# Pools begin at multiples of 512 bytes; the odd tile of attention has a place of its own, network items run in halves

## Chip, core and metric

One core of a Trainium2 chip. The metric is the device time of one execution in microseconds, median of three. TensorE (PE) multiplies and transposes, its weight loads (PEld) are recorded by themselves; ScalarE is ACT, VectorE DVE, GpSimd POOL, SyncE SP.

## What is computed

Linear attention without softmax, its result normalised by its root mean square and laid out by token; then two networks behind each other.

```python
kv  = einsum('bhsd,bhse->bhde', k, v)          # 4 x 8 heads, 576 tokens, 64 wide
out = einsum('bhsd,bhde->bhse', q, kv)
x   = out / sqrt(mean(out**2, -1) + 1e-6) * g_norm     # then 2304 tokens x 512
h = x @ w_in                                   # 512 x 2048
x = (h * clip(h + 3, 0, 6) / 6) @ w_out        # 2048 x 512
p = domain_probs / (domain_probs.sum(-1) + 1e-9)
out = sum(p[:, e] * (maximum(x @ w1[e], 0) @ w2[e]) for e in range(4))   # 512 x 1024 x 512
```

## The kernel before

Each matrix product is split: an operand is held as a rounded part and the rest (names with H and L, or index 0 and 1), and three of the four products are summed. Most matmuls have a type of four bytes, F32R; those of the attention are plain F32.

**Attention.** Eight passes `i`, each for half of the heads of one batch. The order of TensorE, ScalarE and VectorE is written out by hand (`manual_schedule`), so each engine runs its instructions in the order of the program text. A pass is:

- `att_out(i)`: products with the transposed q, 32 calls at L241 and 8 at L248, into `pp`, which has three banks of PSUM and one buffer. ScalarE squares them (L253), VectorE sums (L255).
- `att_q(i+1)`: transposes of the next q (L204, L206) into `pq` and `kvp`; ScalarE copies them out (L208, L212).
- `att_rms(i)`: small instructions (L270 to L278), then VectorE scales `pp` into `xt` (L265).
- `att_kv(i+1)`: the next kv, 72 small matmuls (L223); ScalarE copies it four times into `kvd` (L228).
- in passes 3, 5 and 7 a network item: `ff_in`, 12 matmuls of 512 columns into `ph` (L316 to L318), then ScalarE and VectorE by turns (L324, L325, L327, L328). In the other passes there is none.
- `att_x(i-1)`: transposes of the result of the pass before, four tokens' groups at a time into two tiles `px` (L298), and the odd ninth group into `px8` (L301), which is a corner of `pp`. For each of the three ScalarE writes the rounded part `xH` (L290) and VectorE the rest `xL` (L291).
- `conv(SLOTS[i])`: some steps of converting weights of the first network (`convert`, L145 to L166) from raw tiles that SP loads. One half tile is nine steps, ScalarE's or VectorE's.

A last half pass (`i` = 8) has `att_x(7)` alone. `warm(k)` issues matmuls on zeros.

**First network.** `step` issues per item 12 matmuls that stream `xH` or `xL` (L316 to L318) and 12 that stream `gH` or `gL` (L346); 16 features' groups, four blocks of 512 tokens and one of 256. Conversion goes on beside it under a budget.

**Second network.** 48 rounds: `quad` has seven products of six matmuls with 384 columns that stream `xs` (L690), `outs` 36 matmuls with 512 columns that stream `wout` (L657). `sums` is a tile of VectorE's and ScalarE's for them.

PSUM: `psa` has two buffers under one tag for `pq`, `px`, `ph` and zeros; `psx` one for `pq` and `px`; `psk` holds `kvp`.

Places in a partition: pools are laid out from the left and from the right. On the left, behind constants and a pad of `PADL` words, lie `accp` (acc), `gp` (gH, gL), `rp`, `xp` and `xp0` or `xsp` (xH, xL, xs, sums); in the program before they begin 384 bytes past a multiple of 512 (`gp` at 46464, `xsp` at 91520), and all their tiles are multiples of 512 bytes long. On the right lie `wp` (weights, `wout`) and `winp`, which begin at multiples of 512.

Of the kernel before, what the change touches and what calls it, by code (L numbers as in the profile page):

```python
# [17 lines left out]
def kernel(  # L18
# [46 lines left out]
    PADL, PADR = 48, 248  # L65
# [16 lines left out]
    psa = ctx.enter_context(tc.tile_pool(name="psa", bufs=2, space=bass.MemoryType.PSUM))  # L82
# [51 lines left out]
    def convert(n):  # L134
# [4 lines left out]
        for h in range(2):  # L139
# [20 lines left out]
            nc.vector.tensor_tensor(out=r, in0=r, in1=xf, op=ALU.mult)  # L160
            yield 600
            nc.vector.tensor_tensor(out=r, in0=r, in1=a.bitcast(F32), op=ALU.add)
            yield 600
# [27 lines left out]
    px8 = pp[:, NG * D:NG * D + P]  # L191

    def att_q(i):
# [5 lines left out]
        pq = [pool.tile([P, 2, CJ // 2, CP], F32, tag=tag, name="pq") for pool, tag in ((psx, "x"), (psa, "a"))]  # L199
# [15 lines left out]
    def att_kv(i):  # L215
# [4 lines left out]
        for j in range(CJ):  # L220
            for x in range(2):
                for r in range(NP):
                    nc.tensor.matmul(  # L223
                        kvp[half[x ^ r], r, :D], lhsT=t["k"][half[x], r, j, :], rhs=t["v"][half[x], r, j, :],
                        start=(j == 0), stop=(j == CJ - 1))
        for y in range(2):
            for c in range(2):
                nc.scalar.activation(out=kvd[i % 2][half[y], c], in_=kvp[half[c], :, :D], func=AF.Copy)  # L228
# [3 lines left out]
    def att_out(i):  # L232
# [3 lines left out]
        for jj in range(CJ // 4):  # L236
            for r in range(NP):
                for x in range(2):
                    for y in range(2):
# [4 lines left out]
                            rhs=kv[half[y], x ^ r, r], start=True, stop=True)  # L244
# [37 lines left out]
    def att_x(i):  # L282
# [11 lines left out]
        for r, (pool, tag) in enumerate(((psx, "x"), (psa, "a"))):  # L294
            px = pool.tile([P, TB], F32, tag=tag, name="px")
# [15 lines left out]
    def ff_in(u, t, f, later=False):  # L311
        n = BLK[t][1]
        w = W[u, f][:, 0].rearrange("p j (c f) -> p j c f", c=KD)
        ph = psa.tile([P, TB], F32, tag="a", name="ph")[:, :n]
        for c in range(KD):
            nc.tensor.matmul(ph, lhsT=w[:, 0, c, :], rhs=xH[t][:, c, :], start=(c == 0), stop=False)  # L316
            nc.tensor.matmul(ph, lhsT=w[:, 0, c, :], rhs=xL[t][:, c, :], start=False, stop=False)  # L317
            nc.tensor.matmul(ph, lhsT=w[:, 1, c, :], rhs=xH[t][:, c, :], start=False, stop=(c == KD - 1))  # L318
        gH = gp.tile([P, TB], F32R, tag="gH", name="gH")[:, :n]
# [74 lines left out]
    cv = [0, None]  # L394

# [28 lines left out]
    zero = wp.tile([P, DM], mybir.dt.bfloat16, tag=f"w{NW - 1}", name="zero")  # L424
    nc.vector.memset(zero, 0.0)
    zp = psa.tile([P, DM], F32, tag="a", name="zp")

    def warm(k):
        for _ in range(k):
            nc.tensor.matmul(zp, lhsT=zero[:, :P], rhs=zero, start=True, stop=True)  # L430

    warm(8)
# [13 lines left out]
    FILLS = (3, 5, 7)  # L446
    SLOTS = {0: 4, 1: 2, 2: 2, 3: 1, 4: 2, 5: 1, 6: 2, 7: 1, 8: 4}
# [375 lines left out]
```

## Time and profile before

| what | value |
|---|---|
| median of three runs | 1259.22 us (1256.66 to 1260.12) |
| the profiled execution | 1259.21 us |
| its span, first to last instruction | 1257.4 us |
| mean granted clock of TensorE | 0.982 |
| PE, PEld, DVE, ACT, POOL busy | 97%, 85%, 61%, 47%, 0% |

A busy share is the part of the span in which an engine had at least one instruction under way; a granted clock of 1.00 is 2.4 GHz and one of 0.50 is 1.2 GHz. Times are counted from the span's start. The end of a matmul is modelled and overlaps the next one; its pace is read from starts.

### The profile page before, as it was taken

The numbers are of one execution on the slowest core, as the hardware profiler recorded it, in microseconds if no ns is written. First come the engines' busy times: TensorE is split into PE (matmuls) and PEld (weight loads), VectorE is DVE, ScalarE is ACT, GpSimd is POOL, SyncE is SP. The second block draws the span as 40 slices with busy tenths as digits, with TensorE's granted clock in tenths as the row PEclk, the third lists the DMA queues.
The fourth block names the chain that finished last, engine by engine and source line by source line (L and its number), as shares of the span: only waits on it lengthen the run. The fifth ranks groups of instructions, "written<-read, shape, count | busy, mean of one in ns | idle before, by whom it ended". The sixth has DMA issues, their size and how long they took to land.

```text
span 1257.4 us, 16871 instructions
## 1 busy us (share of the span) xinstructions
PE 1225.7 (97%) x6725; PEld 1073.7 (85%) x6725; DVE 773.3 (61%) x1458; ACT 587.0 (47%) x1129; POOL 1.1 (0%) x10
## 2 busy tenths in 40 slices
PE   7879999999999999999999999999999999999997
PEld 5767788888888889999999998999999899999996
DVE  5556999994353375465656576656565856565652
ACT  5546655552232243444444454444444644444441
POOL 0000000000000000000000000000000000000000
PEclk8779999999999999999999999999999999999999
DMA  9421222220010001111212132122222322222202
GB/s 343 142 73 34 84 68 84 84 84 1 1 68 1 1 1 67 35 68 67 68 67 68 68 96 89 68 67 70 71 71 71 91 90 71 72 72 69 72 8 50
DMA packets 59342, 87.13 MB, mean 69 GB/s; under 512 B 3712, under 2 KB 36480, under 8 KB 59264
## 3 DMA queue, kind: packets, MB, share of 16 engines
q1 hardware_dynamic: 59264, 86.07, 20.8%
q8 instruction: 52, 0.85, 0.3%
q14 instruction: 26, 0.21, 0.1%
HBM read 81.34 MB, written 4.72 MB: 68 GB/s over the span
## 4 chain that ended last, share of the span: by engine, by line
PE 94%; DVE 3%; ACT 2%; DMA 0%; issue 0%; SPq 0%; ACTq 0%; DVEq 0%
PE po L657 31%; PE po L346 15%; PE qa L690 14%; PE qb L690 14%; PE ph L316 5%; PE ph L317 5%; PE ph L318 5%; PE pp L241 2%; PE pq L204 1%; DVE xl L291 1%; PE kvp L223 1%; DVE acc L673 1%; ACT kvd L228 0%; ACT acc L360 0%; DMA qin<-in_q_dram 0%; PE pp L248 0%
## 5 line engine op out<-in xcount | busy, mean ns | idle before, releaser
L657 PE MATMUL po<-wout,g 128*128 128x512 f32 x1728 | 400.9, 389 | 0.0
L657 PEld LDWEIGHTS po<-wout,g 128*128 128x128 f32 x1728 | 323.7, 188 | 64.1
L690 PE MATMUL qb<-xs,win 128*128 128x384 f32 x1008 | 204.6, 338 | 1.2 <-ACT us L731 1.2
L690 PE MATMUL qa<-xs,win 128*128 128x384 f32 x1008 | 204.3, 338 | 0.0
L346 PE MATMUL po<-gH,w 128*128 128x512 f32 (+1 forms) x640 | 196.5, 372 | 1.1 <-DVE xl L291 1.1
L690 PEld LDWEIGHTS qb<-xs,win 128*128 128x128 f32 x1008 | 179.2, 188 | 4.0 <-ACT us L731 1.8
L690 PEld LDWEIGHTS qa<-xs,win 128*128 128x128 f32 x1008 | 179.4, 188 | 2.2 <-ACT us L731 0.2
L564 DVE TENSOR_TENSOR wout<-raw,wout 128x512 fp32r<-128x512 f32 x96 | 62.3, 689 | 170.8 <-ACT wout L563 170.8
L563 ACT ACTIVATE wout<-raw 128x512 fp32r<-128x512 f32 x96 | 55.5, 625 | 226.2 <-PE po L657 226.2
L346 PEld LDWEIGHTS po<-gH,w 128*128 128x128 f32 x640 | 116.9, 188 | 24.4 <-DVE xl L291 1.5
L324 ACT ACTIVATE r<-ph,three 128x512 f32<-128x512 f32 (+1 forms) x80 | 51.7, 646 | 153.2 <-PE ph L318 153.2
L316 PE MATMUL ph<-xh,w 128*128 128x512 f32 (+1 forms) x320 | 120.6, 377 | 0.8 <-DVE r L325 0.8
L318 PE MATMUL ph<-xh,w 128*128 128x512 f32 (+1 forms) x320 | 119.9, 375 | 0.0
L317 PE MATMUL ph<-xl,w 128*128 128x512 f32 (+1 forms) x320 | 119.9, 375 | 0.0
L346 PE MATMUL po<-gL,w 128*128 128x512 f32 (+1 forms) x320 | 119.1, 372 | 0.0
L325 DVE SCALAR_TENSOR_TENSOR r<-r,ph 128x512 f32<-128x512 f32 (+1 forms) x80 | 50.6, 632 | 101.1 <-ACT r L324 101.0
L720 DVE SCALAR_TENSOR_TENSOR g<-sums,g 128x384 fp32r<-128x384 f32 x96 | 53.6, 558 | 81.4 <-ACT g L717 81.4
L717 ACT ACTIVATE g<-cs 128x384 fp32r<-128x384 f32 x96 | 50.5, 526 | 64.1 <-DVE cs L733 55.0
L563 ACT ACTIVATE win<-sums 128x512 fp32r<-128x512 f32 x96 | 60.7, 633 | 40.1 <-DVE sums L576 37.7
L316 PEld LDWEIGHTS ph<-xh,w 128*128 128x128 f32 x320 | 60.8, 190 | 13.3 <-DVE r L325 1.2
L318 PEld LDWEIGHTS ph<-xh,w 128*128 128x128 f32 x320 | 60.7, 190 | 12.0 <-DVE w L166 0.4
L317 PEld LDWEIGHTS ph<-xl,w 128*128 128x128 f32 x320 | 60.8, 190 | 11.7
(99 smaller groups left out, 1260.3 us busy)
## 6 DMA issues: line engine op xcount, KB each, us to landing
raw<-in_moe_w_dram SPq DMA_DIRECT2D x96, 512.0 KB, 4.1
raw<-in_moe_w_in_dram SPq DMA_DIRECT2D x16, 512.0 KB, 3.6
raw<-in_moe_w_out_dram SPq DMA_DIRECT2D x16, 512.0 KB, 3.5
qin<-in_q_dram SPq DMA_DIRECT2D x8, 576.0 KB, 4.9
kin<-in_k_dram SPq DMA_DIRECT2D x8, 576.0 KB, 6.1
vin<-in_v_dram SPq DMA_DIRECT2D x8, 576.0 KB, 7.1
out_dram<-acc SPq DMA_DIRECT2D x36, 128.0 KB, 2.3
dp<-in_moe_domain_probs_dram SPq DMA_DIRECT2D x2, 36.0 KB, 5.5
```

The source lines that it names most:

```text
L316: nc.tensor.matmul(ph, lhsT=w[:, 0, c, :], rhs=xH[t][:, c, :], start=(c == 0), stop=False)
L317: nc.tensor.matmul(ph, lhsT=w[:, 0, c, :], rhs=xL[t][:, c, :], start=False, stop=False)
L318: nc.tensor.matmul(ph, lhsT=w[:, 1, c, :], rhs=xH[t][:, c, :], start=False, stop=(c == KD - 1))
L324: lambda: nc.scalar.activation(out=r, in_=ph, func=AF.Relu, bias=three[:, 0:1]),
L325: lambda: nc.vector.scalar_tensor_tensor(out=r, in0=r, scalar=6.0, in1=ph, op0=ALU.min, op1=ALU.mult),
L346: nc.tensor.matmul(po_t[u, t][o], lhsT=lhsT, rhs=rhs, start=(f == 0 and m == 0), stop=(f == UF[u] - 1 and m == 2))
L563: nc.scalar.activation(out=dst[0], in_=src, func=AF.Copy)
L564: nc.vector.tensor_tensor(out=dst[1], in0=src, in1=dst[0].bitcast(F32), op=ALU.subtract)
L657: nc.tensor.matmul(ps[i], lhsT=lhsT, rhs=w[:, f, y], start=(j == 0 and f == 0 and m == 0), stop=(j == FP - 1 and f == 1 and m == 2))
L690: nc.tensor.matmul(bank, lhsT=w[:, wy, AOP[m], c], rhs=xs[m][:, xy, c], start=first and n == 0, stop=n == 5, skip_group_check=True)
L717: nc.scalar.activation(out=g[f][:, 0, t], in_=src, func=func)
L720: nc.vector.scalar_tensor_tensor(out=g[f][:, 1, t], in0=src, scalar=0.0, in1=g[f][:, 0, t].bitcast(F32), op0=ALU.max, op1=ALU.subtract)
```

## The change

`PADL` grows from 48 to 208 words, 640 bytes, so the left pools begin at multiples of 512 bytes; nothing on the right moves. In the attention:

- the odd ninth group is transposed into columns 256 to 383 of the next pass's `kvp`, no longer into `pp` (in the last pass still into `pp`, and the two `px` into `psk`);
- `psa` has two tags: `a1` for `pq` and `px`, `a0` for `ph` and zeros (afterwards `ph` takes both by turns);
- network items for blocks 0 to 2 are issued in halves: six matmuls in an even pass, the other six and the engines' part in the next; passes 0 and 1 have matmuls on zeros there, of the widths in the diff, and zeros are F32R now;
- one copy of the full height and two of half height go to `kvd`, which were four;
- 30 conversion steps in eight passes, which were 19 in nine. In five half tiles the multiply and the add are GpSimd's, in one step;
- the passes are eight; the last `att_x` follows the loop, and the items behind it have another order.

```diff
...
     FMAX = 3.0e38
-    PADL, PADR = 48, 248
+    PADL, PADR = 208, 248
 
...
     rawp = early.enter_context(tc.tile_pool(name="rawp", bufs=3, side="right"))
-    psa = ctx.enter_context(tc.tile_pool(name="psa", bufs=2, space=bass.MemoryType.PSUM))
+    psa = ctx.enter_context(tc.tile_pool(name="psa", bufs=1, space=bass.MemoryType.PSUM))
     attps = ExitStack()
...
             yield 340
-            nc.vector.tensor_tensor(out=r, in0=r, in1=xf, op=ALU.mult)
-            yield 600
-            nc.vector.tensor_tensor(out=r, in0=r, in1=a.bitcast(F32), op=ALU.add)
-            yield 600
+            e = nc.gpsimd if POOLED[0] <= (n, h) < POOLED[1] else nc.vector
+            e.tensor_tensor(out=r, in0=r, in1=xf, op=ALU.mult)
+            if e is nc.vector:
+                yield 600
+            e.tensor_tensor(out=r, in0=r, in1=a.bitcast(F32), op=ALU.add)
+            yield 600 if e is nc.vector else 0
             nc.scalar.activation(out=w[:, h, 0], in_=r, func=AF.Copy)
...
     pp = psp.tile([P, 3 * TB], F32, name="pp")
-    px8 = pp[:, NG * D:NG * D + P]
 
...
         t["q8"] = q8 = qT[:D, 2 * TB:].rearrange("p (r x s) -> p r x s", r=NP, x=2)
-        pq = [pool.tile([P, 2, CJ // 2, CP], F32, tag=tag, name="pq") for pool, tag in ((psx, "x"), (psa, "a"))]
+        pq = [pool.tile([P, 2, CJ // 2, CP], F32, tag=tag, name="pq") for pool, tag in ((psx, "x"), (psa, "a1"))]
         t["kvp"] = kvp = psk.tile([P, NP, TB], F32, tag="k", name="kvp")
...
                         start=(j == 0), stop=(j == CJ - 1))
+        nc.scalar.activation(out=kvd[i % 2][:, 0], in_=kvp[:, :, :D], func=AF.Copy)
         for y in range(2):
-            for c in range(2):
-                nc.scalar.activation(out=kvd[i % 2][half[y], c], in_=kvp[half[c], :, :D], func=AF.Copy)
+            nc.scalar.activation(out=kvd[i % 2][half[y], 1], in_=kvp[half[1 - y], :, :D], func=AF.Copy)
 
...
                             lhsT=t["qm"][half[y], r, x, 2 * jj:2 * jj + 2, :].rearrange("p j s -> p (j s)"),
-                            rhs=kv[half[y], x ^ r, r], start=True, stop=True)
+                            rhs=kv[half[y], x ^ r ^ y, r], start=True, stop=True)
         for x in range(2):
...
 
-    def att_x(i):
+    def att_x(i, pxs, px8):
 
...
 
-        for r, (pool, tag) in enumerate(((psx, "x"), (psa, "a"))):
-            px = pool.tile([P, TB], F32, tag=tag, name="px")
+        for r in range(NP):
+            px = pxs[r]
             for a in range(HH):
...
 
-    def ff_in(u, t, f, later=False):
+    ph_t = {}
+    ph_n = [0]
+
+    def ff_mm(u, t, f, cs):
         n = BLK[t][1]
         w = W[u, f][:, 0].rearrange("p j (c f) -> p j c f", c=KD)
-        ph = psa.tile([P, TB], F32, tag="a", name="ph")[:, :n]
-        for c in range(KD):
+        if cs[0] == 0:
+            ph_t[u, t, f] = psa.tile([P, TB], F32, tag=f"a{ph_n[0] % 2}", name="ph")[:, :n]
+            ph_n[0] += int(done[0])
+        ph = ph_t[u, t, f]
+        for c in cs:
             nc.tensor.matmul(ph, lhsT=w[:, 0, c, :], rhs=xH[t][:, c, :], start=(c == 0), stop=False)
...
             nc.tensor.matmul(ph, lhsT=w[:, 1, c, :], rhs=xH[t][:, c, :], start=False, stop=(c == KD - 1))
+
+    def ff_in(u, t, f, later=False, cs=(0, 1, 2, 3)):
+        n = BLK[t][1]
+        ff_mm(u, t, f, cs)
+        ph = ph_t.pop((u, t, f))
         gH = gp.tile([P, TB], F32R, tag="gH", name="gH")[:, :n]
...
     cv = [0, None]
+    done = [False]
+    POOLED = ((0, 1), (3, 0))
 
...
 
-    zero = wp.tile([P, DM], mybir.dt.bfloat16, tag=f"w{NW - 1}", name="zero")
-    nc.vector.memset(zero, 0.0)
-    zp = psa.tile([P, DM], F32, tag="a", name="zp")
-
-    def warm(k):
-        for _ in range(k):
-            nc.tensor.matmul(zp, lhsT=zero[:, :P], rhs=zero, start=True, stop=True)
-
-    warm(8)
+    zero = wp.tile([P, DM], F32R, tag=f"w{NW - 1}", name="zero")
+    nc.vector.memset(zero.bitcast(F32), 0.0)
+    def warm(sizes):
+        zp = psa.tile([P, DM], F32, tag="a0", name="zp")
+        for n in sizes:
+            nc.tensor.matmul(zp[:, :n], lhsT=zero[:, :P], rhs=zero[:, :n], start=True, stop=True)
+
+    warm([DM] * 8)
 
...
     nc.sync.dma_start(out=gcol[D:2 * D, :], in_=g_norm.rearrange("(p o) -> p o", o=1))
-    FILLS = (3, 5, 7)
-    SLOTS = {0: 4, 1: 2, 2: 2, 3: 1, 4: 2, 5: 1, 6: 2, 7: 1, 8: 4}
+    SLOTS = {0: 3, 1: 3, 2: 4, 3: 4, 4: 4, 5: 4, 6: 4, 7: 4}
     nop = lambda: None
...
         qc = att_q(0)
-        warm(4)
         for x in qc[:2]:
             x()
+        warm([DM] * 6)
         att_kv(0)
         qc[2]()
+        warm([DM] * 2)
         conv(3)
-        for i in range(NHB + 1):
+        for i in range(NHB):
             if i + 2 < NHB:
...
             nxt = i + 1 < NHB
-            if i < NHB:
-                att_out(i)
-                qc = att_q(i + 1) if nxt else [nop] * 3
-                rms = att_rms(i)
-                qc[0]()
-                rms[0]()
-                qc[1]()
-                for x in rms[1:]:
-                    x()
+            att_out(i)
+            qc = att_q(i + 1) if nxt else [nop] * 3
+            rms = att_rms(i)
+            qc[0]()
+            rms[0]()
+            qc[1]()
+            for x in rms[1:]:
+                x()
             if nxt:
...
                 qc[2]()
-            later = fill(True) if i in FILLS else [nop] * 4
-            later[0]()
-            later[1]()
-            em = att_x(i - 1) if i else []
+            fin = [nop] * 4
+            if i < 2:
+                warm(((480,) * 3 + (504,) * 3 + (506,) * 2, (248,) * 3 + (250,) * 3 + (288,) * 3 + (368,) * 3)[i])
+            elif i % 2 == 0:
+                ff_mm(0, i // 2 - 1, 0, (0, 1))
+            else:
+                fin = ff_in(0, i // 2 - 1, 0, later=True, cs=(2, 3))
+            fin[0]()
+            fin[1]()
+            em = []
+            if i:
+                pxs = [pool.tile([P, TB], F32, tag=tag, name="px") for pool, tag in ((psx, "x"), (psa, "a1"))]
+                em = att_x(i - 1, pxs, st[min(i + 1, NHB - 1)]["kvp"][:, 0, 2 * P:3 * P])
             for m, (x, y) in enumerate(em):
...
                 if m == 1:
-                    later[2]()
+                    fin[2]()
                 y()
-            later[3]()
-            if i < NHB:
-                conv(SLOTS[i])
+            fin[3]()
+            conv(SLOTS[i])
+        pxs = psk.tile([P, NP, TB], F32, tag="k", name="px")
+        for x, y in att_x(NHB - 1, [pxs[:, r] for r in range(NP)], pp[:, NG * D:NG * D + P]):
+            x()
+            y()
+        done[0] = True
         attps.close()
         psb = ctx.enter_context(tc.tile_pool(name="psb", bufs=1, space=bass.MemoryType.PSUM, reuse_waits="tile"))
-        for kind, t in (("o", 0), ("o", 1), ("i", 3), ("i", 4), ("o", 2), ("o", 3), ("o", 4)):
+        for kind, t in (("o", 0), ("i", 3), ("o", 1), ("i", 4), ("o", 2), ("o", 3), ("o", 4)):
             if kind == "i":
...
 
-    qa = psa.tile([P, TB], F32, tag="a", name="qa")[:, :TH]
-    qb = psa.tile([P, TB], F32, tag="a", name="qb")[:, :TH]
+    qa = psa.tile([P, TB], F32, tag="a0", name="qa")[:, :TH]
+    qb = psa.tile([P, TB], F32, tag="a1", name="qb")[:, :TH]
     nc.tensor.matmul(qb, lhsT=win[0][:, 0, 0, 0], rhs=xs[1][:, 0, 0], start=True, stop=True)
...
```

## Rows read from the trace of the kernel before

**Rows 1.** The page: granted clock in 40 slices of the span

```profile
PEclk8779999999999999999999999999999999999999
```

**Rows 2.** Stretches: length, busy (count) of PE, PEld, DVE, ACT, POOL; clock, DMA

```profile
20.50:27.30 6.80, 6.80 (x90) 6.14 (x91) 4.24 (x10) 2.48 (x5) 0.00 (x0) 0.50 1.05 395
...
92.20:99.00 6.80, 6.80 (x46) 5.89 (x44) 2.38 (x8) 2.13 (x4) 0.00 (x0) 0.50 0.00 0
...
110.00:300.00 190.00, 189.25 (x881) 154.94 (x880) 167.84 (x317) 99.46 (x169) 0.00 (x0) 1.00 0.24 73
...
300.00:480.00 180.00, 180.00 (x829) 148.08 (x828) 83.72 (x137) 57.19 (x92) 0.00 (x0) 1.00 0.04 12
```

**Rows 3.** Waits between 11.8 and 106 us: total, times, longest

```profile
PE pp L241 <- DVE xl L291: 14.0, 6, 2.6
```

**Rows 4.** One pass in order of time (start, length)

```profile
31.87 2.00 PE L241 MATMUL pp<-kvd,qT 64*128 64x64 f32 x32 [2.63 <-DVE xl L291]
...
34.93 1.41 DVE L255 TENSOR_REDUCE ssq<-xt 128x8 f32<-128x512 f32 x2 [2.51 <-ACT xt L253]
...
37.82 1.42 DVE L265 TENSOR_TENSOR xt<-pp,ri 128x512 f32<-128x512 f32 x2
...
40.47 1.41 DVE L291 SCALAR_TENSOR_TENSOR xl<-px,gcol,xh 128x512 fp32r<-128x512 f32 x2 [1.23 <-ACT xh L290]
...
41.80 0.34 DVE L291 SCALAR_TENSOR_TENSOR xl<-pp,gcol,xh 128x128 fp32r<-128x128 f32 x1
...
42.19 1.00 PE L241 MATMUL pp<-kvd,qT 64*128 64x64 f32 x14 [2.57 <-DVE xl L291]
```

**Rows 5.** TensorE in order of time: first and eighth pass, output products

```profile
11.77 2.65 PE L241 MATMUL pp<-kvd,qT 64*128 64x64 f32 x32 [0.40 <-ACT kvd L228]
...
91.80 3.36 PE L241 MATMUL pp<-kvd,qT 64*128 64x64 f32 x32 [2.35 <-DVE xl L291]
...
106.15 0.50 PE L346 MATMUL po<-gH,w 128*128 128x512 f32 x1 [1.06 <-DVE xl L291]
```

**Rows 6.** TensorE in order of time, second network

```profile
596.79 1.22 PE L690 MATMUL qa<-xs,win 128*128 128x384 f32 x6
...
603.11 8.34 PE L657 MATMUL po<-wout,g 128*128 128x512 f32 x36
...
611.28 1.21 PE L690 MATMUL qa<-xs,win 128*128 128x384 f32 x6
```

**Rows 7.** TensorE in order of time, first network, 512 columns

```profile
380.90 0.39 PE L316 MATMUL ph<-xh,w 128*128 128x512 f32 x1
...
386.48 0.40 PE L316 MATMUL ph<-xh,w 128*128 128x512 f32 x1
```

**Rows 8.** TensorE in order of time, first network, 256 columns

```profile
334.67 0.28 PE L316 MATMUL ph<-xh,w 128*128 128x256 f32 x1
...
336.09 0.39 PE L346 MATMUL po<-gH,w 128*128 128x512 f32 x1
```

**Rows 9.** TensorE's groups by line and shape, the whole span

```profile
L690 PE MATMUL qb<-xs,win 128*128 128x384 f32 x1008 | 204.6, 338 | 1.2 <-ACT us L731 1.2
...
L346 PE MATMUL po<-gH,w 128*128 128x512 f32 x512 | 171.6, 395 | 1.1 <-DVE xl L291 1.1
```

**Rows 10.** VectorE's conversion by line, 11.8 to 106 us: count, busy, mean ns

```profile
L160 DVE TENSOR_TENSOR r<-r,x 128x512 f32<-128x512 f32 x2 | 1.4, 688 | 0.0
...
L158 DVE TENSOR_SCALAR x<-a 128x512 uint32<-128x512 uint32 x2 | 0.9, 428 | 0.1
```

**Rows 11.** TensorE in order of time: instructions at full clock

```profile
14.73 0.66 PE L204 MATMUL pq<-ident,qin 128*128 128x128 f32 x4
...
15.97 1.28 PE L223 MATMUL kvp<-vin,kin 64*64 64x64 f32 x72
...
100.11 1.03 PE L298 MATMUL px<-ident,xt 128*128 128x128 f32 x8
```

**Rows 12.** GpSimd's groups by line, the whole span

```profile
masks.py:199 POOL TENSOR_SCALAR_AFFINE_SELECT ident<-ident 128x128 f32<-128x128 f32 x1 | 0.3, 295 | 0.0
```

## The prediction

> **What bounds the kernel now.** I read the page first [rows 1]: TensorE's granted clock is whole everywhere except in the first three of the 40 slices (31.4 us each; some 100 us in all), the attention. So there are two questions: where the attention loses time, and at what pace TensorE runs behind it, where it never stops. The busy time of each engine by stretches says the same more sharply [rows 2]: behind 110 us TensorE is busy for 189 of 190 us at clock 1.00, although VectorE has 168 of them full too; inside the attention there are seven stretches at clock 0.50, of which the first and the last are shown, together some 41 of the 89 us between 10.3 and 99.0.
>
> The waits of the attention [rows 3] name the cause: TensorE stands for 14.0 us, six times, before L241 (the products of attention, into `pp`) until VectorE's L291 ends. One pass of the loop in order of time shows which L291 [rows 4]. L241 starts at 31.87, VectorE reduces from 34.93 and has scaled the result at 37.82 + 1.42 = 39.24. Then `pp` could be written again, but the odd tile of the pass before is transposed into a corner of `pp`, and its last reader ends at 41.80 + 0.34 = 42.14. L241 starts at 42.19. A pass is 10.32 us long, of which 2.95 are this detour. In the passes with a network item or a cold clock it is longer: between the first and the eighth L241 (11.77 to 91.80 us) lie 80.0 us, 11.4 a pass [rows 5].
>
> Behind the attention I read TensorE's start times. The second network's second product streams 512 columns from `wout`: 36 of them take 611.28 - 603.11 = 8.17 us, 226.9 ns each; its first one streams 384 columns from `xs`: 36 in 603.11 - 596.79 = 6.32 us, 175.6 ns each [rows 6]. The first network, also 512 columns, streams from `xH`, `xL`, `gH` and `gL`: 24 in 386.48 - 380.90 = 5.58 us, 232.5 ns each [rows 7]. Its short block (256 columns) needs 1.42 us for 12, 118.3 ns each [rows 8]. Between 300 and 480 us VectorE is mostly idle, so the 5.6 ns between the two kinds of 512 columns is no matter of VectorE's load. What differs is the moving operand's place: `wout` begins at a multiple of 512 bytes, and the other four 384 bytes past one. Weights begin at multiples in all of them.
>
> **Part 1, the pads.** 640 more bytes put `x`, `g`, `xs` and `sums` on multiples of 512. The trace has no matmul of 384 or 256 columns that streams from such a place, so both are bounded.
> - 512 columns: 1,500 behind the attention (768 of L346 [rows 9], 768 of L316 to L318, less 36), at 5.6 ns: 8.4 us.
> - 384 columns: 2,016 [rows 9]. If time is in proportion to columns, the aligned one takes 226.9 x 384/512 = 170.2, gain 5.4 ns, 10.9 us. If instead the 128 columns fewer save only their 53.3 ns at 2.4 GHz, it takes 173.6, gain 2.0 ns, 4.0 us. I take 7: the 256-column row is below what a fixed cost on top of 2.4 GHz would give (226.9 - 106.7 = 120.2), so proportion is nearer.
> - 256 columns: 384, between 0 and 118.3 - 113.5 = 4.8 ns: 0 to 1.8 us, I take 1.
>
> The sum is 16.4 us, between 12.4 and 21.1. TensorE is the bound there, so all of it counts; VectorE's 168 of 190 us leave room for steps 2.4% shorter.
>
> One rule of the Trainium skill speaks against this part: "TensorE: Matmul & The Clock Gate", section "Back-to-back issue gap", gives the gap as columns over 2.4 GHz plus 2.5 ns, from the columns alone (215.8 ns for 512), so by it the shift would bring 0 us. The trace does not agree: 226.9 and 232.5 ns for equal columns.
>
> **Part 2, the odd tile.** It goes into the spare columns of `kvp`, so L241 waits for the scaling alone: a pass can't be shorter than 39.24 - 31.87 = 7.37 us. Late next are two queues.
> - VectorE, in order: reduce to scale 4.31 us and the three L291 1.75 [rows 4]; half of a network item's two instructions (L325, L328) every pass, 0.69, as VectorE's instructions with two tiles of 128x512 take 0.69 [rows 10]; conversion. The slots now give the passes from the third on, by turns, L148, L151, L155 and L158 (three at 0.43 and one at 0.69 [rows 10]) and L166 (0.69), 1.3 on the mean. Sum 8.1; with the gaps between instructions and the waits for ScalarE I take 8.5.
> - TensorE at full clock: L241 2.00 [rows 4] and L248 (eight calls more) some 0.4, transposes and L223 15.97 + 1.28 - 14.73 = 2.52 [rows 11], half a network item 6 x 0.2325 = 1.40, and nine transposes of results some 1.1 (eight take 1.03) [rows 11], 7.4 together. At half clock L241 takes 3.36 [rows 5], with L248 some 4.0, the rest at most twice as long, 14.1 together.
>
> So at full clock VectorE sets the pass at 8.5; TensorE's idle time falls from some 3 us a pass to 1, and the clock, which now falls after each such stop, should hold more often. I put a fifth to a quarter of TensorE's time at half clock, which it partly takes out of its 1 us of slack, and take 9.0 (8.3 to 9.9).
>
> **Part 3, small moves.** Two more warming matmuls come ahead of the first L223 (512 columns at 1.2 GHz: 0.43 us each), two more behind it, where TensorE would wait, and one of four copies to `kvd` falls away: the first L241 moves from 11.77 to some 12.4. The warming matmuls of passes 0 and 1 stand where TensorE would wait. Network items in halves are the same 12 matmuls; as `ph` has a bank of its own during attention, transposes no longer wait for its readers. The 11 more conversion steps are VectorE's, counted above; SP's loads behind them wait for instructions that VectorE has executed a pass earlier.
>
> Five half tiles give their multiply and add to GpSimd. No row shows such an operation there. The nearest is a 128x128 select at 0.30 us [rows 12]: four times that, 1.2 us, for 512 columns; ten of them are 12 us. They take 10 x 0.69 = 6.9 us off VectorE [rows 10], which my 8.1 already leaves out. ScalarE's L164 behind them comes a whole pass later, so 2.4 us are covered. If they hold VectorE up for their whole length, the head is 12 us longer; if never, 0. I take 1, since only the tiny instructions between reduce and scale fall in their time.
>
> The Trainium skill ("SBUF — State Buffer", section "Who interferes with whom") says that a VectorE instruction with two SBUF inputs and a GpSimd one that reads SBUF exclude each other for a whole instruction. No row shows it, as GpSimd does nothing here after 2 us; by it the cost is within those bounds.
>
> **Sum for the attention.** First L241 at 12.4; the first pass 7.7 (no L291 yet), six at 9.0: the eighth at 74.1 instead of 91.80. Behind it, before: 106.15 - 91.80 = 14.35, of which 1.4 already went into six output products, so 12.95. After: scaled at 7.37, L325 0.69, the seventh result's L291 1.75, then the last result (transposes 0.45, ScalarE 0.67, L291 1.75): 12.7. Gain 17.9; less 1 for GpSimd, and 1 that I keep back for a first pass at half clock: 16. Bounds: 9.9 us a pass 12, less a part of GpSimd's: 7; 8.3 a pass: 22.
>
> The profiled execution took 1259.21 us (span 1257.4 and 1.8 around it), the median 1259.22. So 1259.2 - 16.4 - 16 = 1226.8, rounded to 1227; with both bounds 1216 to 1240.
>
> **Rivals.**
> 1. The place of the moving operand is not the cause of the 5.6 ns (`wout` also lies at the other end of a partition, beside its weights). For it: no row of the same tile at two places. Against it: `xH` to `gL` lie far apart and all show some 232 ns. Then the attention alone: 1237 to 1252, about 1243.
> 2. The attention gains little, as the clock stays as it was, VectorE's queue is fuller than I count, or GpSimd holds it up: a pass of 11 us. For it: 41 us at 0.50 now. Then 1259.2 - 16.4 and a few us: 1238 to 1247.
> 3. Neither counts: 1256 to 1262.
> 4. Slower. The clock falls in the attention and does not rise again, since half items and products of 64 columns follow each other without long work. Place: L241 of each pass. Price: 14.1 us a pass instead of 11.4, 7 passes, 19 us: 1278 without a gain behind it, 1262 with it. It decides from 11.4 us a pass on without the pads' gain, and from about 13.7 with it. Against it: in every cold stretch of now the clock rose while TensorE was busy throughout [rows 2].
>
> **Chances.** Both parts as said 0.63, the attention alone 0.17, the pads alone 0.10, neither 0.04, slower 0.06. The likeliest gives 1227. From 1215 to 1248 leaves out rivals 3 and 4, and some of 1: less than 2 in 10. Within 0.3% (3.8 us, about what a measurement here can tell from no change) lies rival 3 and a little of rivals 1 and 4: same 0.06; faster 0.89; slower 0.05.
>
> **What would show it.** Start times of L346 at 227 ns each, of L690 at 170 to 174; L241 starting right behind L265 with `pp` no longer waiting for L291; eight passes of 8.3 to 9.9 us; the first output product between 80 and 92 us; at most two or three cold stretches. Wrong would be: 232 ns unchanged, passes of over 10 us, or ScalarE's L164 waiting for GpSimd.

## The result and the profile after

The changed kernel takes 1239.08 us (median of four runs, 1238.81 to 1240.38), the kernel before 1258.11 (four runs, 1256.66 to 1260.12). The ratio is 0.985, with a 95% interval of 0.9832 to 0.9867: faster by 17 to 21 us. The prediction said 1227 with a range of 1215 to 1248. So the sign and the range held: 19 of the 32 us forecast came, and the time is 12 us above the forecast.

The profiled execution took 1240.38 us (span 1238.6). In it TensorE's clock outside the cold stretches is recorded as 0.95, not 1.00; its matmuls keep the same pace as in executions recorded at 1.00, so 0.95 is read here as the upper level. Granted clock in 40 slices, as [rows 1]:

```profile
PEclk9868999999999999999999999999999999999998
```

The waits between 11.8 and 106 us (engine, line and tile; what it waited for; total, times, longest), as [rows 3]:

```profile
POOL r L161 <- DVE x L158: 87.1, 5, 21.0
...
PE px L299 <- DVE xl L292: 6.0, 1, 6.0
...
ACT w L166 <- POOL r L164: 3.9, 1, 3.9
...
PE po L358 <- DVE xl L292: 3.0, 1, 3.0
...
PE pp L242 <- DVE xt L266: 2.4, 2, 1.3
```

The 14.0 us before the products into `pp` are gone: they wait for the scaling (L266) alone, 2.4 us in all. New are three long single stops: 6.0 us before the last transposes, 3.0 before the first output products, and 3.9 of ScalarE waiting for GpSimd. One pass in order of time, as [rows 4] (L266 scales, L292 writes `xl`):

```profile
27.49 2.01 PE L242 MATMUL pp<-kvd,qT 64*128 64x64 f32 x32
...
33.61 1.42 DVE L266 TENSOR_TENSOR xt<-pp,ri 128x512 f32<-128x512 f32 x2
...
35.08 1.11 PE L242 MATMUL pp<-kvd,qT 64*128 64x64 f32 x16
...
35.15 1.41 DVE L292 SCALAR_TENSOR_TENSOR xl<-px,gcol,xh 128x512 fp32r<-128x512 f32 x2
```

The next L242 starts at 35.08, with the end of the scaling, and L292 comes after it. This pass is 7.59 us long; all seven between the first L242 (11.09) and the eighth (71.71) take 8.66 on the mean, against 11.4 before [rows 5]. The eighth starts 20.1 us earlier than before. TensorE from there on:

```profile
75.53 1.06 PE L299 MATMUL px<-ident,xt 128*128 128x128 f32 x8
76.42 0.28 PE L302 MATMUL kvp<-ident,xt 128*128 128x128 f32 x1
82.69 1.97 PE L299 MATMUL px<-ident,xt 128*128 128x128 f32 x8 [5.99 <-DVE xl L292]
84.45 0.42 PE L302 MATMUL pp<-ident,xt 128*128 128x128 f32 x1
87.83 0.76 PE L358 MATMUL po<-gH,w 128*128 128x512 f32 x1 [2.95 <-DVE xl L292]
```

And two of the four cold stretches between 45 and 121 us (length, busy time and count of PE, PEld, DVE, ACT, POOL; clock; DMA), as [rows 2]:

```profile
62.50:69.40 6.90, 6.90 (x107) 6.13 (x106) 5.94 (x14) 4.77 (x12) 0.00 (x0) 0.50 0.01 2
79.60:93.25 13.65, 7.61 (x22) 6.07 (x23) 7.45 (x14) 5.97 (x11) 0.00 (x0) 0.50 0.13 38
```

The second is the longest of the kernel. TensorE had stood since 76.70, 2.9 us, when at 79.6 the granted clock went to its lower level, 1.2 GHz; the eight transposes then take 1.97 us instead of 1.06 (75.53), and twelve output products 93.08 - 87.83 = 5.25 instead of 12 x 0.2267 = 2.72. Equal matmuls further on show how much was lost: near 124 us the changed kernel is some 10 us ahead, no longer 20. It gets 8 of these back in the first network, and is 17.8 ahead at the second network's first output (a group of three L690 at 508.78 against L715 at 491.00) and 18.9 at the end (1249.09 against 1230.22). So the second network, the longest part, brings 1.1.

Behind the attention, the second network (36 products of 512 columns, and 384-column ones ahead of them), as [rows 6]:

```profile
582.04 1.20 PE L715 MATMUL qb<-xs,win 128*128 128x384 f32 x6
583.08 1.21 PE L715 MATMUL qa<-xs,win 128*128 128x384 f32 x6
...
585.16 8.36 PE L682 MATMUL po<-wout,g 128*128 128x512 f32 x36
593.36 1.23 PE L715 MATMUL qa<-xs,win 128*128 128x384 f32 x6
```

The first network, 24 matmuls of 512 columns from one row to the other, as [rows 7]:

```profile
354.66 0.39 PE L323 MATMUL ph<-xh,w 128*128 128x512 f32 x1
...
360.10 0.39 PE L323 MATMUL ph<-xh,w 128*128 128x512 f32 x1
```

and twelve of 256 columns, as [rows 8]:

```profile
329.78 0.28 PE L358 MATMUL po<-gH,w 128*128 128x256 f32 x1
...
331.22 0.40 PE L323 MATMUL ph<-xh,w 128*128 128x512 f32 x1
```

So 5.44 / 24 = 226.7 ns for 512 columns (232.5 before), 1.04 / 6 = 173.3 for 384 and 1.44 / 12 = 120.0 for 256 (118.3 before). Each 128 columns are 53.3 ns, which is 2.4 GHz, and 13.4 ns lie on top whatever the length. Over all starts the mean of the 384-column matmuls went from 176.6 to 175.4 only, as one in sixteen takes 182 or more, and that of the 512-column ones of `wout` rose from 227.1 to 227.8.

The Trainium skill, "TensorE: Matmul & The Clock Gate", section "Back-to-back issue gap", has 2.5 ns on top of the columns for a single matmul at 2.4 GHz. The trace does not agree: these FP32R streams show 13.4 ns, and the place counts, too.

### The profile page after: what moved, and what is told of

Same layout as the page of the kernel before. It is cut to its first block, busy times and chain, and to the rows that moved or that the text cites. A ratio compares the mean times of both kernels' runs of the same rounds, so it can differ in the third digit from the quotient of the medians.

```text
span 1238.6 us, 16911 instructions
## 1 busy us (share of the span) xinstructions
PE 1209.9 (98%) x6749; PEld 1067.7 (86%) x6749; DVE 769.6 (62%) x1448; ACT 583.4 (47%) x1121; POOL 14.0 (1%) x20
## 4 chain that ended last, share of the span: by engine, by line
PE 93%; DVE 3%; DMA 2%; ACT 1%; issue 0%; SPq 0%; POOLq 0%; POOL 0%; ACTq 0%; DVEq 0%
PE po L682 31%; PE po L358 15%; PE qa L715 14%; PE qb L715 14%; PE ph L323 5%; PE ph L324 5%; PE ph L325 5%; DMA vin<-in_v_dram 1%; DMA kin<-in_k_dram 1%; PE pp L242 1%; DVE acc L698 1%; PE kvp L224 1%; DVE xl L292 1%; PE pq L205 0%; PE px L299 0%; ACT acc L372 0%
## 5 line engine op out<-in xcount | busy, mean ns | idle before, releaser
L715 PE MATMUL qb<-xs,win 128*128 128x384 f32 x1008 | 203.3, 336 | 1.2 <-ACT us L756 1.2
L715 PE MATMUL qa<-xs,win 128*128 128x384 f32 x1008 | 203.0, 335 | 0.0
L715 PEld LDWEIGHTS qb<-xs,win 128*128 128x128 f32 x1008 | 177.9, 188 | 3.8 <-ACT us L756 1.8
L715 PEld LDWEIGHTS qa<-xs,win 128*128 128x128 f32 x1008 | 178.2, 188 | 2.2 <-ACT us L756 0.2
L358 PEld LDWEIGHTS po<-gH,w 128*128 128x128 f32 x640 | 118.3, 190 | 26.3 <-issue 3.3
L323 PE MATMUL ph<-xh,w 128*128 128x512 f32 (+1 forms) x320 | 119.6, 374 | 2.4 <-DVE r L337 2.4
L325 PE MATMUL ph<-xh,w 128*128 128x512 f32 (+1 forms) x320 | 118.3, 370 | 0.0
L337 DVE SCALAR_TENSOR_TENSOR r<-r,ph 128x512 f32<-128x512 f32 (+1 forms) x80 | 50.5, 632 | 101.5 <-ACT r L336 101.2
L323 PEld LDWEIGHTS ph<-xh,w 128*128 128x128 f32 x320 | 61.0, 190 | 13.6 <-DVE r L337 2.9
L745 DVE SCALAR_TENSOR_TENSOR g<-cs,g 128x384 fp32r<-128x384 f32 x96 | 53.3, 555 | 27.2 <-ACT g L742 27.2
```

The lines of the kernel that those rows point to most:

```text
L337: lambda: nc.vector.scalar_tensor_tensor(out=r, in0=r, scalar=6.0, in1=ph, op0=ALU.min, op1=ALU.mult),
L358: nc.tensor.matmul(po_t[u, t][o], lhsT=lhsT, rhs=rhs, start=(f == 0 and m == 0), stop=(f == UF[u] - 1 and m == 2))
L715: nc.tensor.matmul(bank, lhsT=w[:, wy, AOP[m], c], rhs=xs[m][:, xy, c], start=first and n == 0, stop=n == 5, skip_group_check=True)
L745: nc.vector.scalar_tensor_tensor(out=g[f][:, 1, t], in0=src, scalar=0.0, in1=g[f][:, 0, t].bitcast(F32), op0=ALU.max, op1=ALU.subtract)
```

## Experiments

My theory: the operand's place gives some 9 us; the odd tile out of `pp` shortens the passes; and about 10 us are given back at the handover by the stop ahead of the last transposes, by the cold clock that it leaves, and by GpSimd's last half tile. Rivals: it isn't the place but the attention's new order that speeds the stream; the halves and the conversion shorten the passes, not the odd tile; ScalarE and VectorE set the handover, not TensorE's clock. All ratios below are to the kernel before, with 95% intervals.

| run | median us | ratio |
|---|---|---|
| the changed kernel | 1239.1 | 0.985 (0.9832 to 0.9867) |
| e1_before_pad832 | 1250.5 | 0.9949 (0.9929 to 0.9969) |
| e2_before_pad704 | 1255.4 | 0.9995 (0.9973 to 1.0017) |
| e3_before_pad64 | 1250.9 | 0.994 (0.9917 to 0.9962) |
| e8_before_pad128 | 1250.3 | one run |
| e4_after_pad192 | 1246.9 | 0.9921 (0.9896 to 0.9946) |
| e12_before_px8_alone | 1241.2 | 0.9843 (0.9807 to 0.9879) |
| e5_after_px8_back | 1254.1 | 0.9968 (0.9954 to 0.9982) |
| e10_after_whole_items | 1246.3 | 0.9898 (0.9881 to 0.9915) |
| e6_after_gpsimd_to_2_0 | 1233.5 | 0.9806 (0.9784 to 0.9827) |
| e11_gpsimd_none | 1240.1 | 0.9855 (0.9838 to 0.9872) |
| e7_after_filled_wait | 1238.6 | 0.985 (0.9833 to 0.9868) |
| e9_gpsimd_filled_own_tiles | 1230.2 | 0.9776 (0.9758 to 0.9793) |

### The pads

```diff
-    PADL, PADR = 48, 248
+    PADL, PADR = 208, 248     # e1 (e2: 176, e3: 16, e8: 32)
```

> The kernel before with one number changed: the left pad has 208 elements instead of 48, so x, g and sums begin at multiples of 512 bytes; attention stays as it was. My theory (a matmul whose moving operand begins off the multiple costs about 6 ns more at 512 columns, 1 to 2 ns more at 384, nothing at 256): 512-column cadence 233 to 227 ns, 384-column 176.5 to 173.5, 256-column unchanged or 1 ns longer, and the time about 1249 us (9 less). Rival, the place is not the cause of the faster cadence (it comes with the attention's new order): about 1258 us.

> The kernel before with a left pad of 176 elements instead of 48: all tiles behind it move by exactly 512 bytes, so that each keeps its remainder to 512. My theory (the remainder counts): no change, 1258 us, 512-column cadence 233 ns. Rival (the amount of the move or the neighbourhood counts, not the remainder): the cadence and the time of the run with 208 elements, about 1249 us.

> The kernel before with a left pad of 16 elements instead of 48: all tiles behind it move down by 128 bytes, to a remainder of 256 to 512. If only the multiple of 512 is free: 1258 us, 512-column cadence 233 ns. If a multiple of 256 is free too: about 1249 us and 227 ns. If the cost grows with what hangs over: between them.

> The kernel before with a left pad of 32 elements: x, g and sums begin 64 bytes beyond a multiple of 256 (before: 128 beyond; the run with 16 elements: on it, at 256 beyond a multiple of 512, and as fast as on the multiple of 512). If only the multiple of 256 is free: a 512-column cadence of 231 to 235 ns. If the remainder's size counts: clearly different from before's 233, in either direction; if 64 is free: 227.

The same 24 matmuls of the first network, in e3:

```profile
382.86 0.39 PE L316 MATMUL ph<-xh,w 128*128 128x512 f32 x1
...
388.30 0.39 PE L316 MATMUL ph<-xh,w 128*128 128x512 f32 x1
```

and in e8:

```profile
383.03 0.39 PE L316 MATMUL ph<-xh,w 128*128 128x512 f32 x1
...
388.52 0.39 PE L316 MATMUL ph<-xh,w 128*128 128x512 f32 x1
```

That is 226.7 and 228.8 ns each on the mean of the 24; e1 has 226.7 (381.19 to 386.63) and e2 232.5 (382.57 to 388.15). So the place is the cause, with the attention untouched, and the amount of the shift isn't: e2 moves everything by 512 bytes and changes nothing. But the multiple is 256, not 512, as e3 shows: 256 bytes past a multiple of 512 is as good. The cost isn't one of on or off either: 128 bytes past a multiple of 256 costs 5.8 ns, 64 bytes past costs 2.1. In e8 the second network even gains more than in the changed kernel (384 columns 174.7 on the mean, `wout`'s 512 columns 227.0, as against 175.4 and 227.8), so that the one run of e8 is as fast as e1 and e3. Why, stays open.

### The attention without the pads

```diff
-    PADL, PADR = 208, 248
+    PADL, PADR = 48, 248
```

> The changed kernel with the left pad of before (48 elements): the attention's part of the change by itself. My theory: 1248 us, that is 10 below the kernel before and 9 above the changed kernel, with the passes of attention as short as in the changed kernel (8.7 us) and the 512-column cadence back at 233 ns. Rival, the place is not the cause: 1239 us.

1246.9 us, 7.8 above the changed kernel, with the pace of before (232.1 to 233.3 ns) and passes of 8.29 us on the mean. The two parts, 6.4 (e1) and 9.9 us (e4, both from the ratios), are 16.3 together, beside 18.9 for the whole; their own intervals, 2.5 and 3.1 us either way, cover the difference.

### The odd tile, alone and put back

On the kernel before (e12) and on the changed one (e5):

```diff
 e12
-    px8 = pp[:, NG * D:NG * D + P]
...
-    def att_x(i):
+    def att_x(i, px8):
...
-            em = att_x(i - 1) if i else []
+            em = att_x(i - 1, st[min(i + 1, NHB - 1)]["kvp"][:, 0, 2 * P:3 * P]) if i else []
 e5
-                em = att_x(i - 1, pxs, st[min(i + 1, NHB - 1)]["kvp"][:, 0, 2 * P:3 * P])
+                em = att_x(i - 1, pxs, pp[:, NG * D:NG * D + P])
```

> The changed kernel with the odd tile's transposes back in the results' tile pp in every pass; the pads and the network items in halves stay. My theory (the move out of pp is what shortens the passes): the wait of L242 for the last xl write returns at 1 to 2 us a pass, a pass takes 10 us or more instead of 8.7, the eighth L242 starts near 81 us instead of 71.7, and the time is about 1248 us. Rival (the halves, and the conversions' place, shorten the passes): passes stay under 9 us and the time under 1242 us.

> The kernel before with one edit: the odd tile's transposes go to the next pass's kvp tile instead of the results' tile pp; pads, network items, conversion's places and engines stay as before. If the move out of pp is by itself what shortens the passes: L241's wait of 14.0 us for the xl writes goes, passes of 11.4 us on average become 9 to 9.5, time about 1244 us (14 less, which is what putting the tile back cost the changed kernel). Rival (the move pays only together with the halves and GpSimd's share, because TensorE then waits without work and falls to half clock, and VectorE's queue is longer): passes of 10 us or more, 1250 us or more.

In e5 the wait is back (the view of waits):

```profile
PE pp L242 <- DVE xl L292: 11.6, 6, 2.1
```

Its eighth L242 starts at 89.09 and its time is 15 us longer than the changed kernel's, more than I had expected. e12 goes further: one edit, with old pads, old items and no GpSimd, gives as much as the whole change as far as the intervals tell (15 to 24 us, the whole change 17 to 21). No L240 (L241 before) waits for an `xl` write any more. TensorE in three of its passes:

```profile
50.09 2.00 PE L240 MATMUL pp<-kvd,qT 64*128 64x64 f32 x32
...
57.52 2.00 PE L240 MATMUL pp<-kvd,qT 64*128 64x64 f32 x32 [0.35 <-DVE xt L264]
...
67.82 2.00 PE L240 MATMUL pp<-kvd,qT 64*128 64x64 f32 x32
...
75.42 2.36 PE L240 MATMUL pp<-kvd,qT 64*128 64x64 f32 x32 [0.35 <-DVE xt L264]
```

7.4 and 7.6 us where the pass has no network item, 10.3 where it has one; the pass with an item ahead of these took 11.77, and all seven take 9.16 on the mean, within the 9 to 9.5 expected. The eighth starts at 75.42 and the first output product at 89.70, later than in the changed kernel (71.71 and 87.83); yet the profiled execution, at 1246.13 us the slowest of its four, has gained 13.5 us by 120 us, against 10. And e12 (1241.2) lies below e4 (1246.9), which has the same pads and everything else of the change besides; their intervals don't meet. So by the medians the rest of the attention's part, taken together, costs time; the two profiled executions don't show it, as e4's has gained 14.2 us by 120 us. The next runs take the rest apart.

### The halves of the network items

```diff
             elif i % 2 == 0:
-                ff_mm(0, i // 2 - 1, 0, (0, 1))
+                pass
             else:
-                fin = ff_in(0, i // 2 - 1, 0, later=True, cs=(2, 3))
+                fin = ff_in(0, i // 2 - 1, 0, later=True)
```

> The changed kernel with the network items whole in passes 3, 5 and 7, as in the kernel before, and none in passes 2, 4 and 6. My theory (VectorE's queue sets the pass, TensorE has some 1 us to spare, so that whole items lengthen an odd pass by less than they shorten an even one): the passes stay at 8.6 to 9 us and the time within 2 us of the changed kernel's 1239. Rival (the halves carry the clock and the passes): TensorE cold in the passes without an item, passes of 9.5 us or more, time 1243 us or more.

The rival won: 1246.3 us. Stretches from one L242 to the next, a pass with a whole item and one without:

```profile
37.40:49.20 11.80, 11.80 (x145) 10.36 (x145) 7.51 (x17) 4.97 (x13) 2.54 (x2) 0.71 0.62 216
49.20:57.50 8.30, 6.46 (x133) 5.33 (x132) 7.28 (x16) 7.87 (x18) 0.00 (x0) 1.00 0.64 223
```

In the second TensorE is busy for 6.46 of 8.30 us, at 1.00; the pass behind such a one begins at half clock (mean 0.71) and takes 11.8 us, TensorE busy throughout. Both kinds together are 10.05 a pass; with the halves the same four passes take 9.16 (35.08 to 71.71). It is the clock: VectorE is busy for only 7.51 of the 11.80. Not all of the 7.2 us between the medians need be the halves: in this profiled execution the first L242 already starts 1.8 us later (12.89 against 11.09), ahead of every pass that the edit touches, and near 130 us it is 6.1 us behind the changed kernel in all.

### GpSimd's half tiles

```diff
 e6
-    POOLED = ((0, 1), (3, 0))
+    POOLED = ((0, 1), (2, 1))
 e11: the same, and
-            e = nc.gpsimd if POOLED[0] <= (n, h) < POOLED[1] else nc.vector
+            e = nc.vector
+            pooled = POOLED[0] <= (n, h) < POOLED[1]
...
-            if e is nc.vector:
+            if not pooled:
                 yield 600
...
-            yield 600 if e is nc.vector else 0
+            yield 0 if pooled else 600
```

> The changed kernel with GpSimd's share ending one half tile earlier, so that the half tile behind the loop over passes, (2, 1), goes back to VectorE. My theory (GpSimd's 2.7 us there delay ScalarE's L166, the copies of the sums behind it, and TensorE): L166's wait of 3.9 us shrinks by about 1.5 us, TensorE's waits near 103 and 117 us (1.6 and 2.5 us) shrink by as much together or more, time about 1236 us (2 to 4 less than the changed kernel). Rival (VectorE loses 1.3 us by it and gives nothing back): 1239 us or more.

> The changed kernel with GpSimd's share ended before (2, 1) and its four other half tiles put on VectorE in the same steps, so GpSimd computes nothing there. Against the run with the share cut alone (1233.5 us): each half tile puts 1.4 us back on VectorE, which my theory has as what sets the pass, so the four passes lengthen by up to 1.4 us each and the time goes to 1235 to 1239 us. Rival (VectorE's small operations are slowed by GpSimd at the same port as much as its work shrinks, or the pass is set elsewhere): 1233 us or less.

GpSimd takes 1.28 us an operation (its groups by line, changed kernel), as estimated:

```profile
L164 POOL TENSOR_TENSOR r<-r,a 128x512 f32<-128x512 f32 x5 | 6.4, 1280 | 0.4
L161 POOL TENSOR_TENSOR r<-r,x 128x512 f32<-128x512 f32 x5 | 6.4, 1278 | 87.1 <-DVE x L158 87.1
```

The last half tile in order of time, changed kernel:

```profile
98.83 0.42 DVE L158 TENSOR_SCALAR x<-a 128x512 uint32<-128x512 uint32 x1
...
99.39 1.29 POOL L161 TENSOR_TENSOR r<-r,x 128x512 f32<-128x512 f32 x1 [21.01 <-DVE x L158]
...
100.77 1.28 POOL L164 TENSOR_TENSOR r<-r,a 128x512 f32<-128x512 f32 x1
...
102.08 0.63 ACT L166 ACTIVATE w<-r 128x512 fp32r<-128x512 f32 x1 [3.89 <-POOL r L164]
```

ScalarE comes to L166 at 98.19 and stands until 102.08; behind it wait the copies of the sums (L372), for these TensorE (1.6 us near 103), and later TensorE again for VectorE's L337 (2.5 us at 117.3), after which its clock is low until 120.6. In e6 VectorE has L164 done at 98.50 + 0.69, ScalarE's L166 follows at 99.22 after a wait of 0.60, and both of TensorE's waits are gone:

```profile
99.22 0.63 ACT L166 ACTIVATE w<-r 128x512 fp32r<-128x512 f32 x1 [0.60 <-DVE r L164]
```

Taking one half tile of five off GpSimd was worth 5.5 us, more than I expected. The other four are better there: e11 is 6.6 us slower than e6. VectorE's queue isn't the only reason: it is longer by 1.4 us in those passes, but three passes take 10.7 to 11.4 us, where e6's take 8.9 (L243, which is L242 here, from 45.26 to 55.97, 67.38 and 78.10). The first and the third of them run at full clock nearly throughout (means 0.95 and 1.00). In them ScalarE stands 2.58 and 2.34 us for VectorE's half tile (L167, which is L166 here; all its waits up to 122 us below), and TensorE behind it 2 us for ScalarE's copies. Only in the one between is the clock low: it fell at 54.8 us, within the first one's stops, and rose at 65.0.

```profile
ACT w L167 <- DVE r L165: 8.9, 5, 2.6
```

### The wait filled, and tiles of their own

```diff
 e7, in the last pass, behind att_x(i - 1) (e9: 18 products)
+            if not nxt:
+                for _ in range(24):
+                    nc.tensor.matmul(st[i]["kvp"][:, 1, :], lhsT=W[0, 0][:, 0, 0, :P],
+                                     rhs=xH[0][:, 0, :], start=True, stop=True)
 e9, behind the loop, with e6's POOLED
-        pxs = psk.tile([P, NP, TB], F32, tag="k", name="px")
-        for x, y in att_x(NHB - 1, [pxs[:, r] for r in range(NP)], pp[:, NG * D:NG * D + P]):
+        pxs = [pool.tile([P, TB], F32, tag=tag, name="px") for pool, tag in ((psx, "x"), (psa, "a1"))]
+        em = att_x(NHB - 1, pxs, pp[:, NG * D:NG * D + P])
+        for _ in range(11):
+            nc.tensor.matmul(pp[:, :TB], lhsT=W[0, 0][:, 0, 0, :P], rhs=xH[0][:, 0, :],
+                             start=True, stop=True)
+        for x, y in em:
```

> The changed kernel with 24 products of 512 columns of real data in TensorE's 6 us of waiting in the last pass, behind the transposes of the result before; they go to the free half of that pass's kvp tile and nobody reads them. My theory (the half clock from 79.6 to 93.3 us comes from that wait and costs the last transposes about 1 us and the first twelve second products 2.3 us): the clock stays up there, L299's eight take 1.1 us instead of 2.0, the twelve products 2.8 instead of 5.1, time about 1236 us (3 less). Rival (what TensorE gains, ScalarE's queue takes back at the copies of the sums): 1239 us.

> The changed kernel with GpSimd's share ending before (2, 1), the last pass's wait filled with 18 products of 512 columns, the gap behind the last transposes filled with 11 more (both into sums that nobody reads), and the last pair of transposed tiles in the two tiles that the other passes use, in place of one shared tile. My theory (the half clock through the handover and the shared tile's waits of 0.8 to 1 us are worth it): against the run with GpSimd's share alone cut (1233.5 us) about 1 us from the last transposes, 2.3 from the first twelve second products and 1 to 1.5 from the tiles, so 1229 us. Rival (ScalarE and VectorE set the handover, TensorE's clock doesn't): 1233 us.

e7 came out at the rival's number. TensorE in order of time:

```profile
77.37 5.72 PE L507 MATMUL kvp<-xh,w 128*128 128x512 f32 x24
83.93 1.09 PE L299 MATMUL px<-ident,xt 128*128 128x128 f32 x8 [0.84 <-DVE xl L292]
84.86 0.27 PE L302 MATMUL pp<-ident,xt 128*128 128x128 f32 x1
88.18 0.77 PE L358 MATMUL po<-gH,w 128*128 128x512 f32 x1 [3.05 <-DVE xl L292]
```

The transposes run at full clock (1.09 us), as I said. But behind the next stop, 3.05 us, the output products start at half clock again. And the fill isn't free: ScalarE's read of the odd tile in `kvp` waits 0.82 us for these products, which go to the same tile. From the eighth L242 (72.67) to the first output product it is 15.5 us, against 16.1. e9 fills both stops and gives the last pair two tiles:

```profile
77.98 1.31 PE L299 MATMUL px<-ident,xt 128*128 128x128 f32 x8 [0.58 <-DVE xl L292]
79.14 0.27 PE L302 MATMUL pp<-ident,xt 128*128 128x128 f32 x1
79.16 2.79 PE L519 MATMUL pp<-xh,w 128*128 128x512 f32 x11
81.79 0.39 PE L358 MATMUL po<-gH,w 128*128 128x512 f32 x1
```

13.5 us from the eighth L242 (68.29) to the first output product, and twelve of these in 84.51 - 81.79 = 2.72 us. The kernel takes 1230.2 us: surely faster than the changed one, by some 9 us; the step from e6 (3.3 us) is smaller than the intervals can tell. Its profiled execution, 1226.0 us, is the fastest of five, and in it the clock stays up from beginning to end (the page's slices):

```profile
PEclk9999999999999999999999999999999999999999
```

In e6 the clock fell in passes 4 and 6 too, and three passes took 8.9 us that take 8.0 to 8.4 here, though the two kernels have the same code up to there. So part of e9's spread (1226.0 to 1232.2) is probably whether a pass turns cold: the mean clock is 0.999 in its fastest execution and 0.994 to 0.996 in the others.

## Why the prediction was right, and where it was off

**Part 1, the pads: cause right, one term wrong.** Rival 1 is refuted by e1, e2 and e3. The 512-column term was right (5.6 ns predicted, 5.8 measured). The 384-column term failed: I took 7 us between 4.0 (fixed cost) and 10.9 (proportion), because the 256-column row lay below what a fixed cost would give. But that row was itself of a misplaced operand; on its multiple it is 120.0, just the 120.2 of the fixed cost. Measured: 1.2 ns x 2,016 = 2.4 us, below even the lower bound. Two terms of the wrong sign came on top: 256 columns cost 0.7 us more (1.7 ns x 384) and `wout`'s products 1.2 us (0.7 ns x 1,728), costed at nothing. The place of `wout` is the same in both kernels, so its 0.7 ns stay open. The sum is 8 to 9 us in the traces and 6.4 in e1's times, where I said 16.4 and at least 12.4.

**Part 2, the odd tile: right.** L242 starts behind L266, as predicted; a pass takes 8.66 (said: 9.0, 8.3 to 9.9), and the eighth starts at 71.71 (said: 74.1). Two of its signs don't fit: the seventh pass, a cold one, took 10.34 us, and there are four cold stretches, not two or three. e5 and e12 show that the tile is the cause. What I didn't foresee is that the rest of the attention's part isn't needed for it: e12 alone comes out level with the whole change.

**Part 3, the small moves: failed at one place.** "ScalarE's L164 behind them comes a whole pass later" (L166 in the changed kernel) holds for four half tiles, which save 6.6 us (e11 against e6); it doesn't for the fifth, behind the loop, where the next step follows at once. This wait, which I had put at nothing and named as a sign of being wrong, costs 5.5 us (e6). The 1 us that I took was for GpSimd holding up VectorE; in VectorE's queue that is 1.9, three L276 of 0.8 us each (last section).

**The sum for the attention: its last term failed.** I counted 12.7 us from the eighth L242 to the first output product; it is 16.1. The last pair of transposed tiles shares one tile of `psk` with the seventh result's odd tile, so it waits until that is read at 82.64, not for the scaling, which ends at 80.46; and in the stop the clock falls, as rival 4 had it for the passes.

```profile
79.04 1.42 DVE L266 TENSOR_TENSOR xt<-pp,ri 128x512 f32<-128x512 f32 x2
...
82.30 0.34 DVE L292 SCALAR_TENSOR_TENSOR xl<-kvp,gcol,xh 128x128 fp32r<-128x128 f32 x1
```

e9, which takes out the shared tile and both stops together, needs 13.5 us here, e6 16.1, and e7, which fills the first stop alone, 15.5; what the tile and the second stop are worth by themselves isn't shown. So 20.1 us at the eighth L242 became some 10 at 124 us: 3.2 went up to the first output product (16.1 against 12.95), 2.5 in the twelve cold products and some 4 in TensorE's two waits behind GpSimd's half tile.

The two shortfalls, 7 to 10 us of the pads and some 6 of the attention (16 predicted, 9.9 in e4), make up the 13 us that are missing of the 32, within what the intervals allow.

Open: why e12 beats e4 in the medians. In the profiled executions e4's eighth pass starts 6.1 us earlier than e12's (69.30 against 75.42), and by 120 us 0.7 of that is left (14.2 against 13.5 us ahead of the kernel before); behind that both keep their lead. So e4 loses some 5 us at the hand-over and at GpSimd's fifth half tile, which alone was worth 5.5 in e6. But e4's profiled execution is the fastest of its four and e12's the slowest: e12's others are 3 to 8 us shorter, with a mean clock of 0.989 to 0.992 instead of 0.985, and which of their passes gain no trace shows. If differences between runs add up, the halves (7.2 us, e10) and the other half tiles (6.6, e11) leave something else in the change that costs time; the 11 more conversion steps in VectorE's queue during attention are what I suspect, but no run has the old steps alone. Nor was e12 run with the new pads. And why the clock falls in one execution's pass and not in another's isn't settled.

## What to carry to other kernels

Move a reader out of the tile that the next pass writes before anything else: here that one edit came out level with the whole change, and what was built around it paid only when the end of the loop was mended as well (e6, e9). Look at the end of a loop by itself: a hand-over to a slower engine that a whole pass covers is bare behind the last pass, and a stop of some microseconds there is paid a second time at half clock. Bound an unmeasured shape by a row of the same condition: the misplaced 256-column row pointed the wrong way.

## What the hardware showed beyond expectation

- A moving operand of FP32R on a multiple of 256 bytes streams at 53.3 ns for 128 columns and 13.4 ns on top; for 512 columns, 64 bytes past the multiple costs 2.1 ns (e8, one run) and 128 bytes past 5.8. At 256 columns 128 bytes past is 1.7 ns faster.
- A tiny VectorE instruction with two inputs takes 0.18 us, but some 0.8 in three of the eight passes, each time while GpSimd's L164 runs (40.29 to 41.58, 57.95 to 59.24 and 77.13 to 78.39). Minimum, median and maximum of its eight, and the slow ones, with GpSimd's in the last pass:

```profile
L276 DVE SCALAR_TENSOR_TENSOR va<-va,r x8: 178/180/836, 16.7 to 77.6; 128x18 f32<-128x18 f32 x8
```

```profile
40.80 0.82 DVE L276 SCALAR_TENSOR_TENSOR va<-va,r 128x18 f32<-128x18 f32 x1
...
58.44 0.84 DVE L276 SCALAR_TENSOR_TENSOR va<-va,r 128x18 f32<-128x18 f32 x1
...
77.13 1.26 POOL L164 TENSOR_TENSOR r<-r,a 128x512 f32<-128x512 f32 x1
...
77.63 0.79 DVE L276 SCALAR_TENSOR_TENSOR va<-va,r 128x18 f32<-128x18 f32 x1
```

They end at 41.62, 59.28 and 78.42, each right behind GpSimd's. In e11, without GpSimd, all eight take 0.18. The Trainium skill, "SBUF — State Buffer", section "Who interferes with whom", says that an instruction of VectorE with two SBUF inputs and a GpSimd one that reads SBUF exclude each other for a whole instruction; this agrees. It costs VectorE 1.9 us in all.
